# A cached-attention decode step with a gated dense branch: the last unit's keys and values in one transfer, and another order in the tail

## The chip, the cores and the metric

The kernel runs on one core of one Trainium2 chip. All numbers are float32. The metric is the device time of one execution in microseconds (us), of which the median of several runs is given. Engines are called as the profile calls them: PE (matrix engine; PEld are its weight loads), DVE (vector), ACT (scalar), POOL (general), SP (here it only issues transfers).

## The reference

Two query rows (batch 2, one position each, 448 features) attend over a cache of 4096 positions with 16 heads of 256, and in parallel go through a dense layer of 1792 hidden features with a relu. A gate mixes the two results.

```python
q = (x @ wq).reshape(B, Sq, H, Dh).transpose(0, 2, 1, 3)
scores = einsum("bhqd,bhkd->bhqk", q, k_cache) * (Dh ** -0.5)
p = softmax(scores, axis=-1)
a = einsum("bhqk,bhkd->bhqd", p, v_cache).transpose(0, 2, 1, 3).reshape(B, Sq, H * Dh) @ wo
b = einsum("bsf,fd->bsd", maximum(einsum("bsd,df->bsf", x, w1), 0), w2)
g = sigmoid((x * gate_w).sum(-1, keepdims=True))
out = g * a + (1 - g) * b
```

## The kernel before

**Units.** One pair of head and batch row is a unit; there are U = 32, numbered 0 to 31. Its keys (transposed) and values lie side by side in one row of `kv`: 128 partitions of 16384 floats, 8 MB, of which the first half of each partition is K and the second half V. The kernel streams all units through `ring`, three slots of that size. Unit u sits in slot (u + 1) mod 3; slot 0 first holds `wq` and the inputs.

**The loop.** For each unit, PE computes the scores `sc` (L131): 16 matmuls in the source, each of them two instructions in the trace, in four column groups side by side, so that the four groups hold four quarters of the 4096 positions. DVE takes the maximum (`nm`, L360), ACT the exponential with its sum (`p` and `ls`, L323), then copies the query columns of a later unit (`qc`, L325). DVE multiplies the values by `p` and sums in eight instructions of 128 x 1024 (L365, into `on`). The last of them raises `freed`, on which three engines wait: SP, to issue the next transfer into that slot; ACT, to copy `on` to this unit's columns of `ov` (L328, the last step of its loop); and PE, after the loop. No running maximum is kept. Each unit has its own maximum and sum in each of the four groups, and they are joined at the end.

**Order of transfers.** SP issues all loads in one queue: `wq`, units 0 to 31, then `wm` in two parts (`w1`, the dense layer's first matrix, 3136 KB; then `w2` and the first eight chunks of `wo`, together 4928 KB), then `wo`'s other 24 chunks. A chunk is 128 rows of a matrix with 448 columns, 224 KB. `wo` comes in five pieces: `ACC` (12 and 4 chunks) and `DIRECT` (5, 2 and 1). Each piece has a semaphore of its own. `w1` and `w2` go into slot 0 when unit 29 has left it; `wo` goes into slot 1 when unit 30 has left it. Unit 31 comes in two transfers, K (L171) and V (L172). The V half has a semaphore `last_v`. DVE waits for it in each step of its loop (L362), with a value that matters only in the last one.

**The tail on PE.** L111 and L114 compute the hidden layer into `pa` (12 chunks of full height, then 2 of half height). Amid them stand the pieces of the joining. The maxima and sums of all units are transposed (L236, L237); DVE takes the least of the negated maxima (`nb`), ACT the exponential (`e`), DVE sums and divides (`el`, `rl`, `wb`); PE spreads these weights over the partitions (L240); DVE scales `ov` to `os`; PE sums its groups (L247); and DVE copies the outcome to `oc`, in the form of weights for the product with `wo`. Then ACT applies the relu to `pa` (`hs`, L332), PE transposes it (L252, L254), and ACT copies it to `hr` (L334, L337). Now come the products: `w2`'s 14 chunks (L260, with `hr`), `wo`'s first 8 chunks (L270, with `oc`) and the 16 of `ACC` (L276), all accumulated in `acc`, chunk k in column group k mod 4. DVE copies `acc` to `a_sb`; PE adds up its four groups into `z` (L283, with `fold`), and the last eight chunks of `wo` (`DIRECT`) go directly into `z` (L288). ACT copies `z` to `res` and issues the output.

Each engine runs its instructions in the order of the source. Only semaphores order one engine against another.

Of the kernel before, what the change touches and what calls it, by code (L numbers as in the profile page):

```python
# [4 lines left out]
AF = mybir.ActivationFunctionType  # L5
# [4 lines left out]
P, HP = 128, 64  # L10
G = 4
R = P // G
SLOTS = 3
CW = 512
EARLY = 8
ACC = (12, 4)
DIRECT = (5, 2, 1)
OUT0, OUTN = 24, 80

# [1 line left out]
def gated_mix_decode(nc, wq, kv, wm, wo, out):  # L21
    U, _, SW = kv.shape
    D = 448
    B = 2
# [4 lines left out]
    J = DH // R  # L29
    KC, KF = 4, 3  # L30
    H = U // B
    HH = H // G
# [7 lines left out]
    pe, dve, act, pool, sp = nc.tensor, nc.vector, nc.scalar, nc.gpsimd, nc.sync  # L40
# [4 lines left out]
    def ev():  # L45
        sems.append(nc.alloc_semaphore(f"e{len(sems)}"))
        return sems[-1]
# [5 lines left out]
    slot = [ring[:, i * SW:(i + 1) * SW] for i in range(SLOTS)]  # L53
# [8 lines left out]

    out_sem = nc.alloc_semaphore("out_sem")
    slot_in = [ev() for _ in range(SLOTS)]
    last_v, w1_in, w2_in = ev(), ev(), ev()
    wo_in = [ev() for _ in ACC + DIRECT]
    scored, maxed, raised, queried, freed, kept = (ev() for _ in range(6))

# [83 lines left out]
    with nc.Block(no_gpsimd_drain=True) as block:  # L152

        @block.sync
        def _(_e):
            sp.wait_ge(fold_ok, 1)
            sp.dma_start(slot[1], kv[0]).then_inc(slot_in[1], 16)
            sp.dma_start(slot[2], kv[1]).then_inc(slot_in[2], 16)
            sp.wait_ge(q_mm, 2)
            sp.dma_start(slot[0], kv[2]).then_inc(slot_in[0], 16)  # L160
            with nc.Fori(0, LOOP - 2, engines=(ET.SP,)) as r:
                u0 = sp.snap(r * SLOTS)
                for k in range(SLOTS):
                    s = (k + 1) % SLOTS
                    sp.wait_ge(freed, u0 + k + 1)
                    sp.dma_start(slot[s], kv[bass.ds(u0 + k + SLOTS, 1)].rearrange("o p n -> (o p) n")  # L166
                                 ).then_inc(slot_in[s], 16)
            sp.wait_ge(freed, U - 4)
            sp.dma_start(slot[1], kv[U - 2]).then_inc(slot_in[1], 16)
            sp.wait_ge(freed, U - 3)  # L170
            sp.dma_start(slot[2][:, :SW // 2], kv[U - 1][:, :SW // 2]).then_inc(slot_in[2], 16)  # L171
            sp.dma_start(slot[2][:, SW // 2:], kv[U - 1][:, SW // 2:]).then_inc(last_v, 16)  # L172
            sp.wait_ge(freed, U - 2)
            sp.dma_start(w1, wm[:, :W1]).then_inc(w1_in, 16)
            sp.dma_start(slot[0][:, W1:wm.shape[1]], wm[:, W1:]).then_inc(w2_in, 16)
            sp.wait_ge(freed, U - 1)
            k = 0
            for n, s in zip(ACC + DIRECT, wo_in):
                sp.dma_start(w_o[:, k * D:(k + n) * D], wo[:, k * D:(k + n) * D]).then_inc(s, 16)  # L179
                k += n  # L180

        @block.gpsimd
        def _(_e):
            pool.memset(ident, 0.0).then_inc(ident_0, 1)
            pool.memset(xl, 0.0).then_inc(xl_0, 1)
            pool.wait_ge(ident_0, 1)
            pool.affine_select(out=ident, in_=ident, compare_op=ALU.not_equal, fill=1.0, base=0, pattern=[[-1, P]],
                               channel_multiplier=1).then_inc(ident_ok, 1)
            pool.memset(qt[:, U, :], 0.0).then_inc(last_v, 1)
            pool.wait_ge(par_ok, 1)  # L190
            pool.tensor_scalar(fold, par[:, None, :].to_broadcast([P, RB, B]), 1.0 / RB, None, op0=ALU.mult
                               ).then_inc(fold_ok, 1)
# [34 lines left out]
        def pe_tail():  # L227
            half = W1 // 2
            def hidden(lo, hi):
                return project(pa, w1, lambda c, g: g // 2 * half + (g % 2 * KF + c) * FG,  # L230
                               lambda i: i * half + 2 * KF * FG, FG, lo, hi)

            pe.wait_ge(w1_in, 16)
            hidden(0, 2)
            pe.wait_ge(freed, U)
            pe.transpose(pc[:U, :P], nm, ident)  # L236
            pe.transpose(pc[:U, P:2 * P], ls, ident).then_inc(ml_tr, 1)  # L237
            hidden(2, KF)
            pe.wait_ge(wb_ok, 1)
            pe.matmul(pb[:, :U], wb.rearrange("u g r -> u (g r)"), ident[:U, :U], start=True,  # L240
                      stop=True).then_inc(wp_mm, 1)
            hidden(KF, KC).then_inc(hid_mm, 1)
            pe.wait_ge(fold_ok, 1)
            pe.wait_ge(os_ok, 1)
            n = HH * B * J
            for g in range(G):
                m = pe.matmul(pc[g * R:(g + 1) * R, :n], sel,  # L247
                              os.rearrange("p u j -> p (u j)")[:, g * n:(g + 1) * n], start=True, stop=True)
            m.then_inc(po_mm, 1)
            pe.wait_ge(hid_ok, 1)  # L250
            for t in range(KF):
                pe.transpose(pb[:, t * P:(t + 1) * P], hs[:, t * P:(t + 1) * P], ident)  # L252
            for j in range(2):
                m = pe.matmul(pb[j * HP:(j + 1) * HP, KF * P:], hs[:, KF * P:], ident, start=True, stop=True)  # L254
            m.then_inc(hid_tr, 1)
            pe.wait_ge(w2_in, 16)
            pe.wait_ge(hr_ok, 1)
            for k in range(NF):
                g = k % G
                pe.matmul(acc[g * R:(g + 1) * R, :D], hr[:, k, :], w2[:, k * D:(k + 1) * D], start=(k < G),  # L260
                          stop=False)

            def o_of(k):
                return oc[:, k // J, k % J].rearrange("p r b -> p (r b)")

            pe.wait_ge(oc_ok, 1)
            n = EARLY + sum(ACC)
            for k in range(EARLY):
                g = k % G
                pe.matmul(acc[g * R:(g + 1) * R, :D], o_of(k), w_e[:, k * D:(k + 1) * D], start=False, stop=False)  # L270
            k = EARLY
            for i, a in enumerate(ACC):
                pe.wait_ge(wo_in[i], 16)
                for _ in range(a):
                    g, at = k % G, (k - EARLY) * D
                    m = pe.matmul(acc[g * R:(g + 1) * R, :D], o_of(k), w_o[:, at:at + D], start=False, stop=(k >= n - G))  # L276
                    k += 1
            m.then_inc(acc_mm, 1)
            for i, a in enumerate(DIRECT):
                if i == 0:  # L280
                    pe.wait_ge(a_ok, 1)
                    for g in range(G):
                        pe.matmul(z[g * R:(g + 1) * R, :DG], fold.rearrange("p r b -> p (r b)"),  # L283
                                  a_sb[:, g * DG:(g + 1) * DG], start=True, stop=False)
                pe.wait_ge(wo_in[len(ACC) + i], 16)
                for _ in range(a):
                    for g in range(G):
                        m = pe.matmul(z[g * R:(g + 1) * R, :DG], o_of(k),  # L288
                                      w_o[:, (k - EARLY) * D + g * DG:(k - EARLY) * D + (g + 1) * DG],
                                      start=False, stop=(k == NO - 1))  # L290
                    k += 1
            m.then_inc(z_mm, 1)
# [7 lines left out]
        def _(_e):  # L300
# [17 lines left out]
            act.wait_ge(qt_ok, 2)  # L318
            act.activation(qc[:, 1, :], qt[:, 0, :], AF.Copy).then_inc(queried, 1)
            qf = qc.rearrange("p s t -> p (s t)")  # L320
            with nc.Fori(0, U, engines=(ET.Activation,)) as u:
                act.wait_ge(maxed, u + 1)
                act.activation(p, sc, AF.Exp, bias=nm[:, bass.ds(u, 1)], accum_out=ls[:, bass.ds(u, 1)]  # L323
                               ).then_inc(raised, 1)
                act.activation(qf[:, bass.ds((u + 2) % SLOTS * T, T)],  # L325
                               qt[:, bass.ds(u + 1, 1), :].rearrange("p o t -> p (o t)"), AF.Copy).then_inc(queried, 1)
                act.wait_ge(freed, u + 1)
                act.activation(ov[:, bass.ds(u, 1), :].rearrange("p o j -> p (o j)"), on, AF.Copy).then_inc(kept, 1)  # L328
            act.wait_ge(nb_ok, 1)
            act.activation(e, pc[:U, 0:P:R], AF.Exp, bias=nb, scale=-1.0).then_inc(e_ok, 1)  # L330
            act.wait_ge(hid_mm, 1)
            act.activation(hs, pa[:, :FG], AF.Relu, scale=omg).then_inc(hid_ok, 1)  # L332
            act.wait_ge(hid_tr, 1)
# [1 line left out]
            for j in range(2):  # L335
# [2 lines left out]
                                   pb[r, KF * P + j * HP:KF * P + (j + 1) * HP].rearrange("p (k r) -> p k r", r=R),  # L338
                                   AF.Copy)
            a.then_inc(hr_ok, 1)  # L340
            act.wait_ge(z_mm, 1)
            act.activation(res, z[:, :DG], AF.Copy).then_inc(res_ok, 1)
            act.wait_ge(res_ok, 1)
# [3 lines left out]
        def _(_e):  # L347
# [9 lines left out]
            with nc.Fori(0, U, engines=(ET.DVE,)) as u:  # L357
# [1 line left out]
                dve.wait_ge(scored, u + 1)  # L359
                dve.tensor_reduce(nm[:, bass.ds(u, 1)], sc, axis=AX.X, op=ALU.max, negate=True).then_inc(maxed, 1)  # L360
                dve.wait_ge(raised, u + 1)
                dve.wait_ge(last_v, (u + 1) // U * 16 + 1)  # L362
                for j in range(J):
                    v = ring[:, bass.ds(v0 + (SW // 2 + j * SG), SG)]
                    m = dve.scalar_tensor_tensor(v, v, 1.0, p, op0=ALU.mult, op1=ALU.mult, accum_out=on[:, j:j + 1])  # L365
# [77 lines left out]
```

## Time and profile before

| | |
|---|---|
| median of 3 runs | 676.04 us (675.84 to 676.61) |
| the profiled execution, its own time | 675.46 us |
| its span, first to last instruction | 674.1 us |
| mean granted clock of PE | 0.668 |
| PE busy | 216.6 us (32%) |
| DVE busy | 339.5 us (50%) |
| ACT busy | 54.4 us (8%) |
| read from memory | 289.54 MB |

The times inside the trace count from the first instruction of the profiled execution, whose own time is 1.4 us longer than its span. A line of the timeline gives the start, the length, the engine, the line of the source, the operation, and what it writes and reads; in brackets stands how long the engine was idle before and whose event ended that. "x32" means that so many instructions in a row were merged. A line of a table by windows gives the stretch, its length, and for each engine the busy time and the number of instructions; then the clock granted to PE (1.00 is full speed), the busy share of the transfer engines and GB/s.

### The profile page before, as it was taken

How to read it: one execution, taken by the hardware profiler on the slowest of the kernel's cores; microseconds unless marked ns; L12 is line 12 of the kernel's file. 1: busy time of each engine (PE TensorE's matmuls, PEld its weight loads, DVE VectorE, ACT ScalarE, POOL GpSimd, SP SyncE). 2: the span in 40 equal slices, each digit the busy share in tenths (PEclk: the TensorE clock that was granted, in tenths of full speed). 3: DMA queues.
4: the chain of work that ended last, by engine and by line, in shares of the span. 5: the costliest groups of instructions: out<-in, count | busy, mean ns of one | idle time of the engine just before them, and what ended most of it. 6: DMA issues, size and time to landing. Idle time of an engine off the chain costs nothing.

```text
span 674.1 us, 4195 instructions
## 1 busy us (share of the span) xinstructions
PE 216.6 (32%) x1291; PEld 52.7 (8%) x1291; DVE 339.5 (50%) x560; ACT 54.4 (8%) x145; POOL 1.1 (0%) x9
## 2 busy tenths in 40 slices
PE   0643212333232213323321233333212333331447
PEld 0210000000000000000000000000000000000112
DVE  0015566454555665454566645446565544556670
ACT  0110000000000000000000000000000000000110
POOL 0000000000000000000000000000000000000000
PEclk9975566676756677676556767765676776656868
DMA  9999999999999999999999999999999999999997
GB/s 381 428 437 436 436 436 436 436 436 436 436 436 436 436 436 436 436 432 436 436 436 436 436 436 436 436 436 436 436 436 436 436 436 436 436 436 404 416 439 312
DMA packets 6003, 289.63 MB, mean 430 GB/s; under 512 B 752, under 2 KB 880, under 8 KB 1136
## 3 DMA queue, kind: packets, MB, share of 16 engines
q1 hardware_dynamic: 5904, 289.55, 99.3%
q8 instruction: 3, 0.05, 0.0%
q10 hardware_dynamic: 96, 0.04, 0.0%
HBM read 289.54 MB, written 0.04 MB: 430 GB/s over the span
## 4 chain that ended last, share of the span: by engine, by line
DMA 68%; DVE 12%; PE 11%; issue 7%; DVEq 1%; ACT 1%; SPq 0%; ACTq 0%; POOL 0%; POOLq 0%
DMA ring<-in_kv 64%; PE sc L131 10%; DVE ring L365 10%; DMA ring<-in_wo 4%; DVE nm L360 2%; DVEq L365 1%; ACT p L323 1%; PE z L288 0%; DVEq L357 0%; DVEq L362 0%; SPq L179 0%; SPq L166 0%; DVEq L360 0%; ACTq L323 0%; ACTq L325 0%
## 5 line engine op out<-in xcount | busy, mean ns | idle before, releaser
L365 DVE SCALAR_TENSOR_TENSOR ring<-ring,p 128x1024 f32 x256 | 295.9, 1220 | 54.8 <-ACT p L323 54.8
L131 PE MATMUL sc<-ring,qc 128*32 128x512 f32 x1024 | 182.7, 879 | 416.1 <-DMA ring<-in_kv 416.1
L360 DVE TENSOR_REDUCE nm<-sc 128x1024 f32 x32 | 39.2, 1224 | 236.9 <-PE sc L131 236.9
L131 PEld LDWEIGHTS sc<-ring,qc 128*32 128x32 f32 x1024 | 41.2, 154 | 557.0 <-issue 552.7
L323 ACT ACTIVATE p<-sc,nm 128x1024 f32<-128x1024 f32 x32 | 35.6, 1113 | 257.8 <-DVE nm L360 257.8
L328 ACT ACTIVATE ov<-on 128x8 f32 x32 | 6.7, 208 | 309.0 <-DVE ring L365 309.0
L365 DVE DVE_READ_ACCUMULATOR ring<-ring,p 128x1 f32 x256 | 20.9, 81 | 0.0
L352 DVE TENSOR_SCALAR ge<-ge 128x1 f32<-128x1 f32 x1 | 0.2, 156 | 21.5 <-ACT ge L310 21.5
L198 PE MATMUL pa<-ring,xr 128*128 128x1 f32 x6 | 1.4, 356 | 21.3 <-ACT xl L306 21.3
L111 PE MATMUL pb<-ring,xr 128*32 128x512 f32 x48 | 8.1, 824 | 0.0
L111 PE MATMUL pa<-ring,xr 128*32 128x448 f32 x24 | 4.0, 784 | 12.1 <-DMA ring<-in_wm 12.1
L384 DVE COPY a_sb<-acc 128x448 f32<-128x448 f32 x1 | 0.6, 623 | 11.9 <-PE acc L276 11.9
L323 ACT ACTIVATION_READ_ACCUMULATOR p<-sc,nm x32 | 6.2, 193 | 0.0
L325 ACT ACTIVATE qc<-qt x32 | 6.1, 192 | 0.0
L260 PE MATMUL acc<-ring,hr 128*32 128x448 f32 x28 | 5.5, 902 | 1.4 <-DMA ring<-in_wm 1.4
L276 PE MATMUL acc<-ring,oc 128*32 128x448 f32 x32 | 3.2, 541 | 0.0
L198 PEld LDWEIGHTS pa<-ring,xr 128*128 128x128 f32 x6 | 1.4, 326 | 21.3 <-ACT xl L306 21.3
L270 PE MATMUL acc<-ring,oc 128*32 128x448 f32 x16 | 2.5, 554 | 0.0
L381 DVE COPY oc<-pc 128x256 f32<-128x256 f32 x4 | 1.4, 417 | 1.7 <-PE pc L247 1.7
L114 PE MATMUL pb<-ring,xl 128*64 128x512 f32 x8 | 2.2, 618 | 0.0
L288 PE MATMUL z<-ring,oc 128*32 128x112 f32 x64 | 2.0, 264 | 0.4 <-DMA ring<-in_wo 0.4
L302 ACT ACTIVATE xr<-ring 128x384 f32<-128x384 f32 x1 | 0.5, 522 | 18.2 <-DMA ring<-in_wq 18.2
(58 smaller groups left out, 27.3 us busy)
## 6 DMA issues: line engine op xcount, KB each, us to landing
ring<-in_kv SPq DMA_DIRECT2D x2, 4096.0 KB, 35.2
ring<-in_wq SPq DMA_DIRECT2D x1, 7174.0 KB, 19.5
ring<-in_wm SPq DMA_DIRECT2D x1, 4928.0 KB, 39.1
ring<-in_wm SPq DMA_DIRECT2D x1, 3136.0 KB, 27.8
ring<-in_wo SPq DMA_DIRECT2D x1, 2688.0 KB, 26.4
ring<-in_wo SPq DMA_DIRECT2D x1, 1120.0 KB, 30.3
ring<-in_wo SPq DMA_DIRECT2D x1, 896.0 KB, 28.1
ring<-in_kv SPq DMA_DIRECT2D x31, 39.6
```

Source lines behind the costliest of these rows:

```text
L111: m = pe.matmul(dst[g * R:(g + 1) * R, :n], x_of(c), w[:, at(c, g):at(c, g) + n], start=(c == 0), stop=False)
L114: m = pe.matmul(dst[i * HP:(i + 1) * HP, :n], xl.rearrange("p j r b -> p (j r b)"), w[:, at_last(i):at_last(i) + n], start=False, stop=True)
L131: m = pe.matmul(sc[g * R:(g + 1) * R, c * CW:(c + 1) * CW], qc[:, s, t:t + 1].to_broadcast([P, R]), slot[s][:, lo:lo + CW], start=(t == 0) ...
L198: m = pe.matmul(pa[:, :1], x_of(c, P) if c < KF else xn[r].rearrange("p r b -> p (r b)"), xg[r, c, B:], start=(c == 0), stop=(c == KC - 1))
L260: pe.matmul(acc[g * R:(g + 1) * R, :D], hr[:, k, :], w2[:, k * D:(k + 1) * D], start=(k < G), stop=False)
L270: pe.matmul(acc[g * R:(g + 1) * R, :D], o_of(k), w_e[:, k * D:(k + 1) * D], start=False, stop=False)
L276: m = pe.matmul(acc[g * R:(g + 1) * R, :D], o_of(k), w_o[:, at:at + D], start=False, stop=(k >= n - G))
L323: act.activation(p, sc, AF.Exp, bias=nm[:, bass.ds(u, 1)], accum_out=ls[:, bass.ds(u, 1)]).then_inc(raised, 1)
L325: act.activation(qf[:, bass.ds((u + 2) % SLOTS * T, T)], qt[:, bass.ds(u + 1, 1), :].rearrange("p o t -> p (o t)"), AF.Copy).then_inc(quer ...
L328: act.activation(ov[:, bass.ds(u, 1), :].rearrange("p o j -> p (o j)"), on, AF.Copy).then_inc(kept, 1)
L360: dve.tensor_reduce(nm[:, bass.ds(u, 1)], sc, axis=AX.X, op=ALU.max, negate=True).then_inc(maxed, 1)
L365: m = dve.scalar_tensor_tensor(v, v, 1.0, p, op0=ALU.mult, op1=ALU.mult, accum_out=on[:, j:j + 1])
```

## The change

It does four things.

1. Unit 31 comes in one transfer like the others. `last_v` goes, and with it DVE's wait in each step of its loop. (The semaphore had also covered the zeroed last row of `qt`; a new one, `qt_0`, does that, and ACT waits for it once, ahead of its loop.)
2. On PE, the hidden layer is computed in one piece, and its transposes come ahead of the joining's. The joining's last matmuls, now in a small function `joined`, stand between `w2`'s fourth and fifth chunk.
3. On ACT, the joining's exponential comes behind the relu and the copies to `hr`.
4. `ACC` is 10 and 6 chunks instead of 12 and 4.

```diff
-ACC = (12, 4)
+ACC = (10, 6)
...
-    last_v, w1_in, w2_in = ev(), ev(), ev()
+    qt_0, w1_in, w2_in = ev(), ev(), ev()
...
-            sp.dma_start(slot[2][:, :SW // 2], kv[U - 1][:, :SW // 2]).then_inc(slot_in[2], 16)
-            sp.dma_start(slot[2][:, SW // 2:], kv[U - 1][:, SW // 2:]).then_inc(last_v, 16)
+            sp.dma_start(slot[2], kv[U - 1]).then_inc(slot_in[2], 16)
...
-            pool.memset(qt[:, U, :], 0.0).then_inc(last_v, 1)
+            pool.memset(qt[:, U, :], 0.0).then_inc(qt_0, 1)
...
             pe.wait_ge(w1_in, 16)
-            hidden(0, 2)
-            pe.wait_ge(freed, U)
-            pe.transpose(pc[:U, :P], nm, ident)
-            pe.transpose(pc[:U, P:2 * P], ls, ident).then_inc(ml_tr, 1)
-            hidden(2, KF)
-            pe.wait_ge(wb_ok, 1)
-            pe.matmul(pb[:, :U], wb.rearrange("u g r -> u (g r)"), ident[:U, :U], start=True,
-                      stop=True).then_inc(wp_mm, 1)
-            hidden(KF, KC).then_inc(hid_mm, 1)
-            pe.wait_ge(fold_ok, 1)
-            pe.wait_ge(os_ok, 1)
-            n = HH * B * J
-            for g in range(G):
-                m = pe.matmul(pc[g * R:(g + 1) * R, :n], sel,
-                              os.rearrange("p u j -> p (u j)")[:, g * n:(g + 1) * n], start=True, stop=True)
-            m.then_inc(po_mm, 1)
+            hidden(0, KC).then_inc(hid_mm, 1)
             pe.wait_ge(hid_ok, 1)
...
             m.then_inc(hid_tr, 1)
+            pe.wait_ge(freed, U)
+            pe.transpose(pc[:U, :P], nm, ident)
+            pe.transpose(pc[:U, P:2 * P], ls, ident).then_inc(ml_tr, 1)
+            pe.wait_ge(hr_ok, 1)
+            pe.wait_ge(wb_ok, 1)
+            pe.matmul(pb[:, :U], wb.rearrange("u g r -> u (g r)"), ident[:U, :U], start=True,
+                      stop=True).then_inc(wp_mm, 1)
+            def joined():
+                pe.wait_ge(fold_ok, 1)
+                pe.wait_ge(os_ok, 1)
+                n = HH * B * J
+                for g in range(G):
+                    m = pe.matmul(pc[g * R:(g + 1) * R, :n], sel,
+                                  os.rearrange("p u j -> p (u j)")[:, g * n:(g + 1) * n], start=True, stop=True)
+                m.then_inc(po_mm, 1)
+
             pe.wait_ge(w2_in, 16)
-            pe.wait_ge(hr_ok, 1)
             for k in range(NF):
                 g = k % G
+                if k == G:
+                    joined()
...
+            act.wait_ge(qt_0, 1)
             with nc.Fori(0, U, engines=(ET.Activation,)) as u:
...
-            act.wait_ge(nb_ok, 1)
-            act.activation(e, pc[:U, 0:P:R], AF.Exp, bias=nb, scale=-1.0).then_inc(e_ok, 1)
             act.wait_ge(hid_mm, 1)
             act.activation(hs, pa[:, :FG], AF.Relu, scale=omg).then_inc(hid_ok, 1)
...
             a.then_inc(hr_ok, 1)
+            act.wait_ge(nb_ok, 1)
+            act.activation(e, pc[:U, 0:P:R], AF.Exp, bias=nb, scale=-1.0).then_inc(e_ok, 1)
...
-                dve.wait_ge(last_v, (u + 1) // U * 16 + 1)
```

The next rows show what stands where on an engine, before and after: the line, the instruction, what it writes and reads, and its size.

ACT, from the last step of its loop (`ov`) to the output's copy (`res`), before:

```order
L328 ACTIVATE ov<-on 128x8
L321 REGISTER_ALU
L321 COMPARE_AND_BRANCH
L330 ACTIVATE e<-pc,nb 32x4
L332 ACTIVATE hs<-pa,omg 128x448
L334 ACTIVATE hr<-pb 128x384
L337 ACTIVATE hr<-pb 64x64 x2
L342 ACTIVATE res<-z 128x112
```

The same place after:

```order
L330 ACTIVATE ov<-on 128x8
L323 REGISTER_ALU
L323 COMPARE_AND_BRANCH
L332 ACTIVATE hs<-pa,omg 128x448
L334 ACTIVATE hr<-pb 128x384
L337 ACTIVATE hr<-pb 64x64 x2
L342 ACTIVATE e<-pc,nb 32x4
L344 ACTIVATE res<-z 128x112
```

The exponential `e` moved behind the copies to `hr`; the relu (`hs`) follows the loop directly in the new order, and stands behind `ov` in both.

PE, from the hidden layer (`pa`) to `wo`'s accumulated chunks (`acc` with `oc`), before:

```order
L111 MATMUL pa<-ring,xr 32x448 x8
L236 MATMUL pc<-ident,nm 32x128
L237 MATMUL pc<-ident,ls 32x128
L111 MATMUL pa<-ring,xr 32x448 x4
L240 MATMUL pb<-ident,wb 128x32
L114 MATMUL pa<-ring,xl 64x448 x2
L247 MATMUL pc<-os,sel 32x64 x4
L252 MATMUL pb<-ident,hs 128x128 x3
L254 MATMUL pb<-ident,hs 64x128 x2
L260 MATMUL acc<-ring,hr 32x448 x14
L270 MATMUL acc<-ring,oc 32x448 x8
L276 MATMUL acc<-ring,oc 32x448 x16
```

The same place after:

```order
L111 MATMUL pa<-ring,xr 32x448 x12
L114 MATMUL pa<-ring,xl 64x448 x2
L236 MATMUL pb<-ident,hs 128x128 x3
L238 MATMUL pb<-ident,hs 64x128 x2
L241 MATMUL pc<-ident,nm 32x128
L242 MATMUL pc<-ident,ls 32x128
L245 MATMUL pb<-ident,wb 128x32
L261 MATMUL acc<-ring,hr 32x448 x4
L252 MATMUL pc<-os,sel 32x64 x4
L261 MATMUL acc<-ring,hr 32x448 x10
L271 MATMUL acc<-ring,oc 32x448 x8
L277 MATMUL acc<-ring,oc 32x448 x16
```

The joining's four steps (`nm`, `ls`, `wb`, `os`) moved behind the transposes of `hs`, and the last of them into `w2`'s chunks.

SP, the end of its queue; lines with a minus are before, lines with a plus after:

```order
 L169 DMA ring<-in_kv 128x16384
-L171 DMA ring<-in_kv 128x8192
-L172 DMA ring<-in_kv 128x8192
-L174 DMA ring<-in_wm 128x6272
-L175 DMA ring<-in_wm 128x9856
-L179 DMA ring<-in_wo 128x5376
-L179 DMA ring<-in_wo 128x1792
+L171 DMA ring<-in_kv 128x16384
+L173 DMA ring<-in_wm 128x6272
+L174 DMA ring<-in_wm 128x9856
+L178 DMA ring<-in_wo 128x4480
+L178 DMA ring<-in_wo 128x2688
```

Unit 31's two transfers became one; of the transfers behind it only `wo`'s first two changed their sizes; the others keep their order.

## The prediction, made before the changed kernel was run

> **What bounds the kernel now.** I read the page's head first, then the chain of waits, then the timeline of the last two units in order of time.
>
> ```profile
> span 674.1 us, 4195 instructions
> DMA packets 6003, 289.63 MB, mean 430 GB/s; under 512 B 752, under 2 KB 880, under 8 KB 1136
> DMA 68%; DVE 12%; PE 11%; issue 7%; DVEq 1%; ACT 1%; SPq 0%; ACTq 0%; POOL 0%; POOLq 0%
> ```
>
> Transfers bound it: 289.63 MB at 430 GB/s fill the span. DVE and PE stand in the chain only because a slot's release issues the transfer that lands two units later. How evenly the units come is seen where PE, idle before, is let go by a landing:
>
> ```profile
> 600.86 5.75 PE L131 MATMUL sc<-ring,qc 128*32 128x512 f32 x32 [14.16 <-DMA ring<-in_kv]
> ...
> 620.18 6.33 PE L131 MATMUL sc<-ring,qc 128*32 128x512 f32 x32 [13.57 <-DMA ring<-in_kv]
> ...
> 629.83 4.93 PE L131 MATMUL sc<-ring,qc 128*32 128x512 f32 x32 [3.32 <-DMA ring<-in_kv]
> ...
> 638.91 2.23 SPq L179 DMA_DIRECT2D ring<-in_wo  x5
> 639.00 0.21 ACT L328 ACTIVATE ov<-on 128x8 f32 x1 [9.65 <-DVE ring L365]
> ...
> 641.73 1.22 DVE L365 SCALAR_TENSOR_TENSOR ring<-ring,p 128x1024 f32 x1 [1.71 <-ACT p L323]
> ...
> 646.89 3.00 PE L111 MATMUL pa<-ring,xr 128*32 128x448 f32 x16 [12.14 <-DMA ring<-in_wm]
> ...
> 651.04 0.28 PE L236 MATMUL pc<-ident,nm 128*32 128x128 f32 x1 [1.15 <-DVE ring L365]
> ```
>
> Units 29 and 30 start 19.32 us apart (620.18 - 600.86). Unit 31, whose K half comes by itself, starts its scores at 629.83, while DVE still works on unit 30, which it frees at 638.91. So unit 31's scores are ready when DVE is, its products start at 641.73, and all units are done at 651.04. That is 7 us before the second matrix of the dense branch lands, and 20 us before the last piece of wo:
>
> ```profile
> 658.52 5.12 PE L260 MATMUL acc<-ring,hr 128*32 128x448 f32 x26 [1.43 <-DMA ring<-in_wm]
> ...
> 665.33 0.16 PEld L276 LDWEIGHTS acc<-ring,oc 128*32 128x32 f32 x8 [0.61 <-DMA ring<-in_wo]
> 665.35 3.20 PE L276 MATMUL acc<-ring,oc 128*32 128x448 f32 x32
> 665.73 0.13 PEld L276 LDWEIGHTS acc<-ring,oc 128*32 128x32 f32 x4 [0.25 <-issue]
> 666.11 0.13 PEld L276 LDWEIGHTS acc<-ring,oc 128*32 128x32 f32 x4 [0.25 <-issue]
> ...
> 668.61 0.62 DVE L384 COPY a_sb<-acc 128x448 f32<-128x448 f32 x1 [11.93 <-PE acc L276]
> ...
> 670.12 1.41 PEld L288 LDWEIGHTS z<-ring,oc 128*32 128x32 f32 x56 [0.67 <-DMA ring<-in_wo]
> 670.12 2.00 PE L288 MATMUL z<-ring,oc 128*32 128x112 f32 x64 [0.43 <-DMA ring<-in_wo]
> 671.72 0.16 PEld L288 LDWEIGHTS z<-ring,oc 128*32 128x32 f32 x8 [0.19 <-DMA ring<-in_wo]
> 672.19 0.26 ACT L342 ACTIVATE res<-z 128x112 f32<-128x112 f32 x1 [14.24 <-PE z L288]
> ```
>
> Every group of the tail (w2, wo's accumulated parts, its direct parts) waits for its own landing. PE follows the queue to 671.7 and the program ends 2.4 us later. Slack is small there: each wait is under 1.5 us.
>
> **The change part by part.** First, the single row. Nothing of unit 31 can start before all of it is there. Its landing follows unit 30's by a whole period, so its scores start at 620.18 + 19.32 = 639.50 instead of 629.83. From there it is a unit like the others, but with nothing left to hide behind:
>
> ```profile
> L131 PE MATMUL sc<-ring,qc 128*32 128x512 f32 x1024 | 182.7, 879 | 416.1 <-DMA ring<-in_kv 416.1
> 117.94 6.57 PE L131 MATMUL sc<-ring,qc 128*32 128x512 f32 x32 [13.32 <-DMA ring<-in_kv]
> ```
>
> The scores of one unit take 182.7 / 32 = 5.71 us in the mean, 4.93 at the least and 6.57 at the most. From the end of unit 30's scores (620.18 + 6.33 = 626.51) to its release (638.91) the maximum, the exponential and eight products took 12.40. So the last release comes at 639.50 + 5.71 + 12.40 = 657.61, less what the removed DVE wait cost:
>
> ```profile
> 165.37 0.10 DVEq L362
> ```
>
> 0.10 us, so 657.5 against 651.04 before: 6.5 us later. In the other 31 units that 0.10 stays hidden behind the transfers. The removed SP issue was hidden too (unit 30 is still coming in), and ACT's new wait on the zeroed `qt` row, before its loop, is for work done at the program's start.
>
> Second, the tail. The hidden-layer matmuls now run in one piece from 646.89, some 6 us, and end while DVE multiplies: free. But the relu that follows them stands on ACT behind the loop, whose last step (`ov`) waits for the release of unit 31. Relu, the transposes of `hs`, the copies to `hr`, the exponential of the joining and everything of PE behind them therefore line up after 657.5. The old pieces give their lengths:
>
> ```profile
> 651.65 0.25 ACT L330 ACTIVATE e<-pc,nb 32x4 f32<-32x4 f32 x1 [0.34 <-DVE nb L370]
> ...
> 652.71 0.43 PE L240 MATMUL pb<-ident,wb 32*128 32x32 f32 x2 [0.39 <-DVE wb L376]
> ...
> 654.75 0.44 PE L247 MATMUL pc<-os,sel 128*32 128x64 f32 x8
> 654.87 0.63 ACT L332 ACTIVATE hs<-pa,omg 128x448 f32<-128x448 f32 x1 [2.97 <-PE pa L114]
> 655.26 1.42 DVE L381 COPY oc<-pc 128x256 f32<-128x256 f32 x4 [1.67 <-PE pc L247]
> 655.56 0.90 PE L252 MATMUL pb<-ident,hs 128*128 128x128 f32 x3 [0.36 <-ACT hs L332]
> ...
> 657.13 0.49 ACT L334 ACTIVATE hr<-pb 128x384 f32<-128x384 f32 x1 [1.63 <-PE pb L254]
> 657.52 0.43 ACT L337 ACTIVATE hr<-pb 64x64 f32<-64x64 f32 x2
> ```
>
> Release to `ov` 0.09, `ov` 0.21, the loop's end 0.1 (estimated; no row shows work behind a last `ov` that was ready): 0.40. Relu to the transposes 655.56 - 654.87 = 0.69; these to the copies 657.13 - 655.56 = 1.57; the copies 657.95 - 657.13 = 0.82 (`nm`, `ls` and `nb` lie beside them); the exponential through `wb` to its matmul 652.71 - 651.65 = 1.06; the matmul 0.43. Together 4.97, so w2's first chunk starts at 657.5 + 5.0 = 662.5 instead of 658.52. The stall on w2's landing goes; what is late instead is PE itself.
>
> From here on PE has all its data ahead of it: the old row of wo's first part waited until 665.33, and the new ten-chunk part lands sooner by two of its twelve chunks. The cut into 10 and 6 I cost at nothing, since PE comes there after both have landed; were PE early, it would be worth about the 0.6 us of that wait. The 14 + 8 + 16 = 38 chunks step by 0.19 (four weight loads, two chunks, in 666.11 - 665.73 = 0.38) at the full clock: 7.2, and 0.35 for the last one's length. The joining's matmuls amid them add 0.44; the `oc` copies (1.42) lie beside the ten chunks of w2 behind them. But PE does not start at the full clock:
>
> ```profile
> 656.50:659.90 3.40, 1.97 (x12) 0.59 (x16) 0.18 (x1) 0.81 (x3) 0.00 (x0) 0.50 0.95 410
> 659.90:663.30 3.40, 3.40 (x24) 0.97 (x20) 0.00 (x0) 0.00 (x0) 0.00 (x0) 0.52 0.98 414
> 663.30:666.75 3.45, 3.45 (x36) 1.04 (x32) 0.00 (x0) 0.00 (x0) 0.00 (x0) 1.00 1.00 421
> ```
>
> The third number from the end is the granted clock: 0.50 and 0.52 through 4.8 us of w2's chunks, then 1.00. Half a clock for 4.8 us costs 2.4; in the scores, where 3.4 is the length at the full clock (half of the 6.8 that an all-slow unit would take, just over the 6.57), a slow start costs 1.5 to 3.1. In the changed tail PE is idle from about 652 to 659 and then works in pieces; I take 2.0, the lower half, because those pieces may already count, and keep 1.0 and 3.1 as ends. The Trainium skill ("TensorE: Matmul & The Clock Gate", Part 1, on the clock gate) says that the gate opens after one busy window of about 3.4 us of a free-running counter and closes after an idle one. The rows agree (0.50 to 1.00 across one boundary), and by its rule the cost would lie between half a window and one, 1.7 to 3.4, and differ from run to run.
>
> Accumulation ends at 662.5 + 7.55 + 0.44 + 2.0 = 672.5, and the copy `a_sb` starts there instead of at 668.61: 3.9 later. Behind it stood waits for landings, 0.43 before the direct parts and 0.19 within, which go; so `res` comes 3.3 later. **The sum: +3.3 us**, from 675.46 for the profiled execution to 678.8. That execution lies 0.58 under the median of the runs, 676.04; on the median it is 679.3.
>
> **The rivals.** *Not slower, because the clock is up.* If PE is granted the full clock when w2 starts, and unit 31's scores take the shortest time seen, 4.93, then 2.0 and 0.78 go: +0.5, 676.5. The mechanism sits at 662.5, and the sign turns from the point where both slow starts together cost under 0.8 (scores above 4.93, plus chunks above 0.19 each). For it: the row below, where PE was at 1.00 from 2.8 us after it had begun at 629.83, the soonest seen; against it: the row at 656.50 above, 0.50 after pieces of just the kind that will precede w2.
>
> ```profile
> 632.60:636.00 3.40, 2.15 (x22) 0.38 (x12) 3.40 (x7) 0.00 (x0) 0.00 (x0) 1.00 1.07 463
> ```
>
> *Not slower, because the queue gains.* Two 4 MB transfers become one. On the page the two slices of their time are the low ones:
>
> ```profile
> GB/s 381 428 437 436 436 436 436 436 436 436 436 436 436 436 436 436 436 432 436 436 436 436 436 436 436 436 436 436 436 436 436 436 436 436 436 436 404 416 439 312
> ring<-in_kv SPq DMA_DIRECT2D x2, 4096.0 KB, 35.2
> ring<-in_wm SPq DMA_DIRECT2D x1, 3136.0 KB, 27.8
> ```
>
> 404 and 416 against 436 lack 52 GB/s over 16.85 us, 0.88 MB, or 2.0 us of transfer. If that came back, unit 31 and all behind it would be 2.0 earlier: +1.3, 677.3, within the noise. Against it: from unit 30's start to w1's (620.18 to 646.89) two halves and w1, 11.60 MB, took 26.71 us, 434 GB/s, and the whole unit before took 19.32, also 434. The slices misplace packets; nothing is lost. The Trainium skill ("DMA: Bandwidth & Descriptors", Rules for kernel authors) advises to merge small transfers into one large; with the queue full, these rows show no gain from it at this size.
>
> *Slower still.* The gate opens a window later, since PE's pieces between 659 and 662 leave it half idle: 3.4 us more at half the clock, +1.7, 681.0. For it: 659.90 above, where a window full of work was still slow. Against it: w2's chunks fill the window from 662.5 on without a break.
>
> **How the numbers follow.** Forecast 72%, gate late 13%, clock up 8%, queue gains 5%, and 2% for both of the last two at once, which alone ends faster (676.5 - 2.0 = 674.5). The forecast's own ends: scores -0.8 and +0.9, slow start -1.0 and +1.1, so 677.5 to 681.3; the range 677.5 to 681.2 holds it and the late gate, and leaves out the 15% that are not slower. A difference under 0.2% (1.35 us) can't be told from none here. Slower by more: 72 + 13 = 85%; within: 8 + 5 = 13%; faster: 2%.
>
> **What the changed profile would show.** Unit 31's scores released by the transfer at about 639.5; the last `ov` at about 657.6, relu right behind it with ACT idle before and the hidden matmuls long done; w2's first chunk at 662.5 released not by a transfer but by `wb` through its matmul; wo's parts without waits for landings; `a_sb` at about 672.5. It is wrong if the relu runs before the last release, if w2 starts under 660, if chunks step by 0.19 from the start, or if a landing still ends the waits at the direct parts.

## The result, and the profile after

| | median | runs |
|---|---|---|
| changed kernel | 678.82 us | 6, 678.35 to 680.1 |
| before, beside it | 675.98 us | 6, 675.63 to 676.61 |
| ratio | 1.0044 | 95% interval 1.0031 to 1.0057 |

The changed kernel is 2.8 us slower. The same kernel run a second time, further down, was 3.7 us slower. The forecast was +3.3.

The page of the changed kernel: its span, the chain of waits by engine and the head of the chain by line.

```profile
span 677.7 us, 4162 instructions
DMA 65%; DVE 12%; PE 12%; issue 6%; another core or an unknown queue 2%; DVEq 1%; ACT 1%; ACTq 0%; POOL 0%; SPq 0%; POOLq 0%
DMA ring<-in_kv 65%; DVE ring L366 10%; PE sc L131 10%; DVE nm L362 2%; PE acc L261 1%; DVEq L366 1%; ACT p L325 1%; PE acc L277 0%; PE z L289 0%; PE acc L271 0%; DVEq L359 0%; PE pb L236 0%; SPq L166 0%; DVEq L362 0%
```

The chain by line of the kernel before, for comparison:

```profile
DMA ring<-in_kv 64%; PE sc L131 10%; DVE ring L365 10%; DMA ring<-in_wo 4%; DVE nm L360 2%; DVEq L365 1%; ACT p L323 1%; PE z L288 0%; DVEq L357 0%; DVEq L362 0%; SPq L179 0%; SPq L166 0%; DVEq L360 0%; ACTq L323 0%; ACTq L325 0%
```

Before, the chain left the units for a wait on `wo`, 4% of the span. That entry is gone, and PE's products (L261, L271, L277) have entered. So the end of the tail is no longer set by a landing. (The 2% under "another core or an unknown queue" are one piece from 45.07 to 59.90, near the start and far from the change.) The changed kernel's timeline shows where the change happens:

```profile
620.60 5.00 PE L131 MATMUL sc<-ring,qc 128*32 128x512 f32 x32 [13.19 <-DMA ring<-in_kv]
...
639.89 5.59 PE L131 MATMUL sc<-ring,qc 128*32 128x512 f32 x32 [14.29 <-DMA ring<-in_kv]
...
647.22 2.46 PE L111 MATMUL pa<-ring,xr 128*32 128x448 f32 x24 [1.74 <-DMA ring<-in_wm]
...
648.45 1.23 DVE L366 SCALAR_TENSOR_TENSOR ring<-ring,p 128x1024 f32 x1 [1.56 <-ACT p L325]
...
649.62 0.97 PE L114 MATMUL pa<-ring,xl 128*64 128x448 f32 x4
...
657.83 0.21 ACT L330 ACTIVATE ov<-on 128x8 f32 x1 [9.50 <-DVE ring L366]
657.99 0.63 ACT L332 ACTIVATE hs<-pa,omg 128x448 f32<-128x448 f32 x1
658.68 0.90 PE L236 MATMUL pb<-ident,hs 128*128 128x128 f32 x3 [8.09 <-ACT hs L332]
...
661.10 0.26 ACT L342 ACTIVATE e<-pc,nb 32x4 f32<-32x4 f32 x1
...
662.25 0.60 PE L245 MATMUL pb<-ident,wb 32*128 32x32 f32 x2 [1.50 <-DVE wb L377]
...
662.78 1.72 PE L261 MATMUL acc<-ring,hr 128*32 128x448 f32 x8
...
669.54 3.51 PE L277 MATMUL acc<-ring,oc 128*32 128x448 f32 x30
...
673.14 0.62 DVE L385 COPY a_sb<-acc 128x448 f32<-128x448 f32 x1 [6.94 <-PE acc L277]
...
674.03 1.72 PE L289 MATMUL z<-ring,oc 128*32 128x112 f32 x64
675.82 0.26 ACT L344 ACTIVATE res<-z 128x112 f32<-128x112 f32 x1 [14.46 <-PE z L289]
```

Read the brackets. Unit 31's scores wait for the transfer, as every unit's did. The hidden layer is done at 650.6, but relu (`hs`) runs only at 657.99, directly behind the `ov` that was held by DVE's last product; PE stood idle 8.09 us for it. From w2's first chunk (662.78) on no row has a bracket that names a transfer: PE itself sets the end. And that stretch is slow in its first half, as the table by windows of the changed kernel shows (busy time of PE, its weight loads, DVE, ACT and POOL; then granted clock, transfer share, GB/s):

```profile
657.20:662.80 5.60, 2.62 (x15) 1.45 (x15) 1.29 (x7) 1.86 (x6) 0.00 (x0) 0.50 0.99 426
662.80:668.00 5.20, 5.20 (x37) 1.56 (x40) 1.84 (x5) 0.00 (x0) 0.00 (x0) 0.52 1.00 421
668.00:673.10 5.10, 5.05 (x52) 1.56 (x44) 0.00 (x0) 0.00 (x0) 0.00 (x0) 1.00 0.47 186
```

The last row's transfer share, 0.47, says the same from the other side: the queue ran dry about half way through it, while PE still had chunks to do.

### The profile page after: what moved, and what is told of

Its sections match the earlier page's. It is cut to its first block, busy times and chain, and to the rows that moved or that the text cites. A ratio compares the mean times of both kernels' runs of the same rounds, so it can differ in the third digit from the quotient of the medians.

```text
span 677.7 us, 4162 instructions
## 1 busy us (share of the span) xinstructions
PE 216.4 (32%) x1291; PEld 53.6 (8%) x1291; DVE 339.6 (50%) x560; ACT 54.4 (8%) x145; POOL 1.1 (0%) x9
## 4 chain that ended last, share of the span: by engine, by line
DMA 65%; DVE 12%; PE 12%; issue 6%; another core or an unknown queue 2%; DVEq 1%; ACT 1%; ACTq 0%; POOL 0%; SPq 0%; POOLq 0%
DMA ring<-in_kv 65%; DVE ring L366 10%; PE sc L131 10%; DVE nm L362 2%; PE acc L261 1%; DVEq L366 1%; ACT p L325 1%; PE acc L277 0%; PE z L289 0%; PE acc L271 0%; DVEq L359 0%; PE pb L236 0%; SPq L166 0%; DVEq L362 0%
## 5 line engine op out<-in xcount | busy, mean ns | idle before, releaser
L131 PE MATMUL sc<-ring,qc 128*32 128x512 f32 x1024 | 186.3, 894 | 424.3 <-DMA ring<-in_kv 424.3
L111 PE MATMUL pb<-ring,xr 128*32 128x512 f32 x48 | 6.9, 716 | 0.0
L261 PE MATMUL acc<-ring,hr 128*32 128x448 f32 x28 | 5.8, 906 | 0.0
L277 PE MATMUL acc<-ring,oc 128*32 128x448 f32 x32 | 3.9, 539 | 0.0
L111 PE MATMUL pa<-ring,xr 128*32 128x448 f32 x24 | 2.5, 543 | 1.7 <-DMA ring<-in_wm 1.7
L271 PE MATMUL acc<-ring,oc 128*32 128x448 f32 x16 | 2.6, 560 | 0.0
```

What stands on the lines that cost most here:

```text
L111: m = pe.matmul(dst[g * R:(g + 1) * R, :n], x_of(c), w[:, at(c, g):at(c, g) + n], start=(c == 0), stop=False)
L131: m = pe.matmul(sc[g * R:(g + 1) * R, c * CW:(c + 1) * CW], qc[:, s, t:t + 1].to_broadcast([P, R]), slot[s][:, lo:lo + CW], start=(t == 0) ...
```

## The experiments

The theory (A): the last release comes 6.5 us later, because unit 31 can't start before all of it is there; relu and what follows it are queued behind that release; and PE then starts w2's chunks at half its clock. Rivals: the new order of the tail costs by itself (B); one row costs in the queue or as such (C). Twelve runs were made, each beside the kernel before on the same chip, in three groups of four on three chips. "Over before" below is the difference of the two medians.

**Unit 31 in halves again, the new tail kept.**

```diff
-            sp.dma_start(slot[2], kv[U - 1]).then_inc(slot_in[2], 16)
+            sp.dma_start(slot[2][:, :SW // 2], kv[U - 1][:, :SW // 2]).then_inc(slot_in[2], 16)
+            sp.dma_start(slot[2][:, SW // 2:], kv[U - 1][:, SW // 2:]).then_inc(last_v, 16)
...
                 dve.wait_ge(raised, u + 1)
+                dve.wait_ge(last_v, (u + 1) // U * 16 + 1)
```

> The changed kernel with unit 31 in two halves again (the wait of DVE comes back too); its new tail and the cut into 10 and 6 stay. Theory A (the cost is the late last release and what is queued behind it): the release is back at about 651, the first chunk of w2 waits for its landing at 658.5 again, and the time is that of the kernel before within 0.5 us, 675.7 to 676.6. Rival B (the new order of the tail costs by itself): 677.5 or more.

Measured: 675.72 against 675.6, ratio 1.0005 (0.9995 to 1.0014). The new tail costs nothing that could be measured when the release is early; B falls. Its timeline:

```profile
651.28 0.21 ACT L330 ACTIVATE ov<-on 128x8 f32 x1 [9.66 <-DVE ring L367]
...
658.92 1.72 PE L262 MATMUL acc<-ring,hr 128*32 128x448 f32 x8 [1.27 <-DMA ring<-in_wm]
```

The last `ov` is back at 651.28, and w2's first chunk waits for its landing again.

**One row, the old tail.** The kernel before with the first of the change's four parts alone.

```diff
-            sp.dma_start(slot[2][:, :SW // 2], kv[U - 1][:, :SW // 2]).then_inc(slot_in[2], 16)
-            sp.dma_start(slot[2][:, SW // 2:], kv[U - 1][:, SW // 2:]).then_inc(last_v, 16)
+            sp.dma_start(slot[2], kv[U - 1]).then_inc(slot_in[2], 16)
...
-                dve.wait_ge(last_v, (u + 1) // U * 16 + 1)
```

> The kernel before with unit 31 in one row and nothing else changed. Theory A: release at about 657.6, and the old tail needs 7.0 us from the release to w2's first chunk (658.0 - 651.0 in the trace of before) where the new one needs 5.0; less 0.44 for the joining's matmuls, which lie ahead of w2 here: 1.5 us slower than the changed kernel, 680.3 (679.5 to 681.3). Rival B (the new tail's order costs): faster than the changed kernel, 676 to 677.5. Rival C (one row costs in the queue, whatever the tail): as the changed kernel, 678.8.

Measured: 680.95, 5.4 us over before (1.0083, 1.0069 to 1.0097). It was expected about 4.3 over before (680.3 less the 675.98 of the first comparison). The direction of A holds: with a late release the old tail is worse than the new one. It came out 1.1 us above the middle of the expectation, at the top end of its range (679.5 to 681.3, or 3.5 to 5.3 over the same 675.98). The timeline shows where most of that lies:

```profile
656.97 0.21 ACT L328 ACTIVATE ov<-on 128x8 f32 x1 [9.50 <-DVE ring L364]
...
657.44 1.72 PE L111 MATMUL pa<-ring,xr 128*32 128x448 f32 x8
...
664.69 5.36 PE L259 MATMUL acc<-ring,hr 128*32 128x448 f32 x26 [1.01 <-ACT hr L337]
```

From `ov` to the first chunk it took 7.7 us. The expectation used 7.0, read from a trace in which the hidden layer's third group (L111) ran at the full clock in 0.96; here it took 1.72 at half the clock (0.50 granted from 655.0 to 658.5). That is 0.8 of the 1.1; the cause of the rest stays open. A length read at one clock doesn't hold at the other.

**Relu ahead of the last release.** ACT's last loop step is written out, so that its wait for the release comes behind relu and the copies to `hr`. (Its copy of a later unit's query columns goes; there is no later unit.)

```diff
-            with nc.Fori(0, U, engines=(ET.Activation,)) as u:
+            with nc.Fori(0, U - 1, engines=(ET.Activation,)) as u:
...
+            act.wait_ge(maxed, U)
+            act.activation(p, sc, AF.Exp, bias=nm[:, U - 1:U], accum_out=ls[:, U - 1:U]).then_inc(raised, 1)
             act.wait_ge(hid_mm, 1)
             act.activation(hs, pa[:, :FG], AF.Relu, scale=omg).then_inc(hid_ok, 1)
...
             a.then_inc(hr_ok, 1)
+            act.wait_ge(freed, U)
+            act.activation(ov[:, U - 1, :], on, AF.Copy).then_inc(kept, 1)
             act.wait_ge(nb_ok, 1)
```

> The changed kernel with ACT's last loop step written out, so that relu and the copies to hr stand ahead of the wait for the last release. Theory A: from the release to w2's first chunk about 2.2 us instead of 5.0, first chunk at about 659.9, and with the landings as the next bound 2.5 us less than the changed kernel: 676.3 (675.8 to 677.2). Rival C (the queue lost time with the single row): as the changed kernel, 678.8.

Measured: 676.07 against 675.6, 1.0005 (0.9996 to 1.0014): nearly all of the loss is gone, with one row and the release as late as in the changed kernel. Its timeline:

```profile
650.31 0.63 ACT L334 ACTIVATE hs<-pa,omg 128x448 f32<-128x448 f32 x1 [2.39 <-PE pa L114]
...
657.41 0.21 ACT L344 ACTIVATE ov<-on 128x8 f32<-128x8 f32 x1 [4.63 <-DVE ring L370]
...
659.95 1.72 PE L261 MATMUL acc<-ring,hr 128*32 128x448 f32 x8
...
669.97 0.62 DVE L389 COPY a_sb<-acc 128x448 f32<-128x448 f32 x1 [6.60 <-PE acc L277]
```

The first chunk starts 2.5 us after `ov`; in the changed kernel it was 4.95. The rest of the tail still runs with the slow start (10.0 from first chunk to `a_sb`). From the first chunk on no row of this trace waits for a transfer, so PE still sets the end: `res` comes at 672.65, 0.46 later than the 672.19 of before, which agrees with the 0.5 that is left of the loss.

**The clock kept up.** The changed kernel with 44 matmuls on PE whose results nobody reads, in the gaps in which it stood idle.

```diff
+            def awake(n):
+                for k in range(n * G):
+                    g = k % G
+                    pe.matmul(spare[g * R:(g + 1) * R, :FG], x_of(0), w1[:, :FG], start=True, stop=True)
+
             hidden(0, KC).then_inc(hid_mm, 1)
+            awake(9)
             pe.wait_ge(hid_ok, 1)
...
             pe.transpose(pc[:U, P:2 * P], ls, ident).then_inc(ml_tr, 1)
+            awake(2)
             pe.wait_ge(hr_ok, 1)
```

> The changed kernel with matmuls whose results nobody reads on PE: 36 behind the hidden layer (some 6.8 us at the full clock, ending before the last release) and 8 more before the wait for wb. Theory A with its slow start of 2 us: w2's chunks run at the full clock from the start, 2.0 to 2.5 us less than the changed kernel, 676.6 (676.0 to 677.3). If the slow start is not what costs: 678.8. If these matmuls stand in the way: 679 or more.

Measured: 675.93 against 675.6, 1.0005 (0.9996 to 1.0014); a second time 675.82 against 675.55. Its windows and three rows of its timeline:

```profile
650.20:657.20 7.00, 7.00 (x74) 2.24 (x72) 7.00 (x13) 0.00 (x0) 0.00 (x0) 1.00 0.91 388
657.20:661.80 4.60, 3.17 (x29) 1.33 (x27) 1.18 (x7) 1.86 (x6) 0.00 (x0) 1.00 1.01 433
661.80:669.70 7.90, 7.85 (x85) 3.12 (x84) 1.84 (x5) 0.00 (x0) 0.00 (x0) 1.00 0.97 403
```

```profile
657.72 0.21 ACT L338 ACTIVATE ov<-on 128x8 f32 x1 [9.50 <-DVE ring L374]
...
661.83 0.96 PE L269 MATMUL acc<-ring,hr 128*32 128x448 f32 x8
...
669.73 0.63 DVE L393 COPY a_sb<-acc 128x448 f32<-128x448 f32 x1 [5.35 <-PE acc L285]
```

The release is as late as in the changed kernel (`ov` 657.72 against 657.83), and the order behind it is the same. Only the clock differs: 1.00 throughout. `ov` to the first chunk takes 4.1 instead of 4.95, first chunk to `a_sb` 7.9 (669.73 - 661.83) instead of 10.4 (673.14 - 662.78). That is 3.3 us, about the whole loss. Here too no row behind the first chunk waits for a transfer; `res` comes at 672.48, 0.29 later than before. The time lies just under the expected range (676.0 to 677.3); counted over before, 2.5 of the 2.8 us went, the top of the 2.0 to 2.5 expected.

**V first.** As the first experiment, with the two halves issued in the other order.

```diff
+            sp.dma_start(slot[2][:, SW // 2:], kv[U - 1][:, SW // 2:]).then_inc(last_v, 16)
             sp.dma_start(slot[2][:, :SW // 2], kv[U - 1][:, :SW // 2]).then_inc(slot_in[2], 16)
-            sp.dma_start(slot[2][:, SW // 2:], kv[U - 1][:, SW // 2:]).then_inc(last_v, 16)
```

> The run with halves and the new tail (675.7), but with the V half issued ahead of the K half, so that the transfers stay two and the scores can only start when all of unit 31 is there. Theory A (what counts is when K is there): scores at about 639.6, release at 657.7, the time of the changed kernel, 2.9 us over before (2.2 to 3.6). Rival C (the form, one row, is what costs): as before, within 0.5 us.

Measured: 680.16, 4.7 us over before (1.0065, 1.0051 to 1.0079). Two transfers, and yet at least as slow as with one: what counts is when K is there, and C falls as far as it means the form of the transfer. It lies about 1 us above the expected range. Its trace has scores of 6.48, where the changed kernel's had 5.59, and 10.73 from first chunk to `a_sb`, where that had 10.36: slow starts nearer their upper end, 1.3 us together. DVE's wait for the V half is back too.

**The cut of `wo`'s accumulated parts.** The changed kernel with `ACC = (12, 4)`.

> The changed kernel with the accumulated parts of wo cut into 12 and 4 again. Theory A: PE comes to both parts after they have landed, so nothing changes: 2.9 us over before (2.4 to 3.4). If the cut helps: up to 0.6 us more than that, 3.5 over before; if it hurts: less than 2.4.

Measured: 680.68, 5.2 us over before (679.43 to 680.91 in five runs), 1.8 more than the top of what A allowed. Its trace shows no wait for `wo`. Either the cut mattered in a way that the trace doesn't show, or something else had moved. So it was run again, beside the changed kernel, and both once more with the clock kept up:

> The changed kernel itself, beside the next three, because the cut into 12 and 4 gave 680.7 where 678.5 was expected, though its trace shows no wait for wo. If the spread comes from where the clock's rise falls (theory A): runs spread over 678.3 to 681, as those of the cut did, and the two medians differ by less than 1. If the cut into 10 and 6 saves time: a median near 678.5, about 2 us under the next run.

> The changed kernel with 12 and 4 chunks once more. Theory A (the cut does nothing, the clock's rise moves both): within 1 us of the run ahead of it, either way. If the cut costs: about 2 us over it again.

> The run with the clock kept up, with 12 and 4 chunks. With the clock's rise out of the way a cost of the cut must show by itself. Theory A: 0.3 us over before as with 10 and 6, within 0.4 us of the next run. PE comes to the first part sooner here, at about 666.0, when twelve chunks are to have landed at about 664.9. If the cut costs: 1 us or more over the next run.

> The run with the clock kept up, 10 and 6 chunks, as the neighbour of the one before it: 0.3 us over before (0.1 to 0.6).

| | median | over before |
|---|---|---|
| 10 and 6 (changed kernel) | 679.23 us | 3.7 us (1.0055, 1.0041 to 1.0068) |
| 12 and 4 | 678.84 us | 3.3 us (1.0046, 1.0032 to 1.0059) |
| 12 and 4, clock kept up | 676.14 us | 0.6 us (1.0006, 0.9997 to 1.0015) |
| 10 and 6, clock kept up | 675.82 us | 0.3 us (1.0005, 0.9996 to 1.0014) |

This time 12 and 4 is the faster of the two, and with the clock kept up they differ by 0.3 us with intervals that overlap. Side by side, the cut does nothing that could be measured. What had moved the first time stays open. The runs of 12 and 4 spread from 678.3 to 680.91 over the two occasions, but the two sets don't overlap (679.43 and more, 679.33 and less). They ran on different chips, and on the chip of the first set, where V first too came out about 1 us above its expectation, the changed kernel itself was not run: the chip is a rival that these runs can't rule out. The changed kernel run again reached 680.19, not the 681 that theory A expected. The profiled runs of the changed kernel and of the cut show what moves: from first chunk to `a_sb` 10.36 and 10.15 with 10 and 6, 10.62 and 10.27 with 12 and 4. That is half a microsecond, and the scores of unit 31 (5.18 to 6.11 in the same four) add up to 0.9. The slowest runs were not the profiled ones, so it is not shown that these two make up the whole spread of 2.6.

**Every unit in halves.** The kernel before with 32 transfers more.

```diff
+            def unit_in(s, u):
+                sp.dma_start(slot[s][:, :SW // 2], u[:, :SW // 2]).then_inc(slot_in[s], 16)
+                sp.dma_start(slot[s][:, SW // 2:], u[:, SW // 2:]).then_inc(slot_in[s], 16)
...
-            sp.dma_start(slot[1], kv[0]).then_inc(slot_in[1], 16)
+            unit_in(1, kv[0])
```

> The kernel before with every unit in two transfers (unit 31 in three), 32 transfers more; PE waits for both. From the start of unit 30's scores to w1's landing the traces with two halves took 26.72 and 26.71 us and those with one row 26.61 to 26.64: some 0.09 us a transfer. If that is its price: 32 x 0.09 = 2.9 us over before (2.0 to 4.0). If a further transfer in a full queue is free: within 0.5 us. If it costs the 2.0 us that the low slices of the page suggested: over 60 us.

Measured: 676.92, 1.4 us over before (1.0020, 1.0011 to 1.0029): 1.4 / 32 = 0.04 us for a further transfer in a full queue, half of the 0.09 expected and under the expected range (2.0 to 4.0 us in all), and nothing like the 2.0 of the rival.

**One row, and only the joining behind the release.** Relu as in the third experiment, 28 filling matmuls, and the joining's last two steps later among w2's chunks.

```diff
+            awake(7)
             pe.wait_ge(freed, U)
...
                 if k == G:
+                    spread()
+                if k == 2 * G:
                     joined()
```

> The changed kernel (one row) with nothing left behind the last release but the joining: relu and the copies to hr ahead of it, 28 matmuls that nobody reads to keep PE's clock up, w2's chunks at their landing, the weights' matmul between the fourth and the fifth chunk and the joining's sums before the ninth. Theory A: PE waits for landings again and the queue sets the end, with one transfer fewer than before: 0.1 us under before (from 0.4 under to 0.3 over). If a late release itself can't be hidden: 0.5 or more over.

(`spread` holds the wait for `wb` and its matmul.) Measured: 675.62 against 675.51, 1.0000 (0.9991 to 1.0009). Its timeline has landings in the brackets again:

```profile
659.06 0.96 PE L272 MATMUL acc<-ring,hr 128*32 128x448 f32 x8 [1.48 <-DMA ring<-in_wm]
...
667.46 1.70 PE L288 MATMUL acc<-ring,oc 128*32 128x448 f32 x12 [0.61 <-DMA ring<-in_wo]
...
671.75 0.16 PEld L300 LDWEIGHTS z<-ring,oc 128*32 128x32 f32 x8 [0.21 <-DMA ring<-in_wo]
672.21 0.26 ACT L359 ACTIVATE res<-z 128x112 f32<-128x112 f32 x1 [14.15 <-PE z L300]
```

Its `res` comes at 672.21, where before had 672.19. A late release can be hidden in full, and nothing is won by it: the landings set the end again, at the same time. No version tried beats the kernel before.

## Why the prediction was right

Term by term, from the changed kernel's rows. Its units came 0.4 later than in the trace of before (620.60 against 620.18), so lengths are compared, not times.

- *Unit 31 starts a whole period after unit 30*: 19.32 forecast, 639.89 - 620.60 = 19.29 measured.
- *Scores to the last release*: 18.0 forecast to the release (657.5 - 639.5), which is 18.1 to `ov`; 657.83 - 639.89 = 17.94 measured. The removed DVE wait was worth a little more than its 0.10: DVE's idle time before unit 31's products fell from 1.71 to 1.56.
- *Release to the first chunk*: 4.97 forecast, of it 4.88 from `ov` on; 4.95 measured. That relu was stuck behind the last `ov` is shown by the experiment that moved it: first chunk 2.8 us earlier, all but 0.5 us of the loss gone.
- *The slow start*: 2.0 taken, with ends at 1.0 and 3.1. This term was a little small, and the reason for taking the lower half did not hold: the pieces ahead of w2 did not bring the full clock any sooner; it was 0.50 amid them and 0.52 in the 5.2 us behind. Against the run with the clock kept up the stretch from first chunk to `a_sb` is 10.36 - 7.90 = 2.5 us longer; the pieces between release and first chunk lost another 0.8, which the forecast had inside its 4.97, since their rows were slow ones too. The estimate of 1.7 to 3.4 from the 3.4 us window of the Trainium skill ("TensorE: Matmul & The Clock Gate", Part 1) holds this 2.5.
- *Behind `a_sb`*: 2.96 forecast, 675.82 - 673.14 = 2.68 measured. The old rows held a little more waiting than was taken off.
- *The cut into 10 and 6*: nothing forecast, nothing found. *The hidden layer in one piece*: it took 3.4 us, not 6, at the full clock, but hidden either way.

The slips cancel: from first chunk to `a_sb` +0.4 (10.36 against 7.55 + 0.44 + 2.0 = 9.99), behind `a_sb` -0.3, scores to `ov` -0.2, the rest under 0.1. The mechanism was right; that the sum comes out to 0.1 is luck, since the six runs of this one kernel lie up to 1.75 us apart. So `res` is 675.82 - 672.19 = 3.6 later, less 0.4 for the later start of the stream: 3.2, against 3.3. (The range ends at 681.2, 0.1 short of the forecast's own upper end, 681.3; nothing hangs on it.)

Of the rivals, "the clock is up" was the right mechanism on a condition that this kernel doesn't meet. When its first half, the full clock for w2, was made by hand, the time came out at 0.3 over before, where the rival had 0.5. That it agrees so well is luck: the other half, scores of 4.93, was not met (5.78 in that trace), and in its place the pieces ahead of the first chunk became 0.8 shorter. "Slower still" did not come: by it, first chunk to `a_sb` would have taken about 11.7 (9.99 + 1.7); 10.36 was measured, and 10.73 in V first was the longest of any trace. "The queue gains" was wrong by its price: 0.04 us a transfer in the run with every unit in halves, 0.09 from unit 30's scores to the hidden layer's start (647.22 - 620.60 = 26.62, against 26.71 before), not 2.0; the low slices of the page did not stand for lost time. What the whole change is made of is seen from its parts alone: the single row with the old tail cost 5.4 us, the new tail by itself nothing, both together 2.8 to 3.7.

## What to carry to other kernels

When transfers set the pace, the last tile is the one whose compute nothing hides: split it so that its first consumer can start early (worth 5.4 us here with the old tail), or see to it that nothing but its own dependants is queued behind its release. An engine that runs in order makes independent work (here relu) wait for the last step of a loop ahead of it; write that step out, and put the independent work ahead of its wait. And read lengths at the clock at which they will run: w2's first four chunks took 0.96 us where the gaps ahead of them had been filled, and 1.72 where PE had stood idle.

## What the runs showed of the hardware that was not expected

Matmuls that nobody reads paid for themselves: 44 of them, in gaps of 8 and 1.5 us, took 2.5 us (2.8 - 0.3, against the first comparison) and 3.4 us (679.23 - 675.82, side by side) off the changed kernel's time, where 2.0 to 2.5 was expected. The pieces of real work ahead of w2's chunks did not raise the clock (2.62 us busy in 5.60, granted 0.50); with the gaps filled, it was 1.00 beforehand, and 3.17 us busy in 4.60 held it there.

A further transfer cost 0.04 us in a queue that did not run empty: 32 of them, from cutting 8 MB transfers into two of 4 MB (one of 4 MB into two of 2), cost 1.4 us.
